# Three moves in SP's order: the store, the loads and the products of the blocked logits transposes

## The chip, the cores and the metric

One core of a Trainium2 chip runs the whole kernel. The metric is device time in microseconds, the median of three runs; smaller is better.

## The reference

Three stages follow one another on 4608 tokens of 512 features.

```
attn:  block-causal softmax(q k^T / 8) v,     8 batches, 8 heads, 576 positions, head size 64
moe:   x = relu(x @ w_in)**2 @ w_out          w_in 512 x 2048, w_out 2048 x 512
moe2:  logits = x @ phi                       phi 512 x 32
       d = softmax of logits over the tokens;  slot_input = d.T @ x
       slot_out[e] = relu(slot_input[e] @ w1[e]) @ w2[e]     8 experts, 4 slots each
       out = softmax of logits over the slots @ slot_out
```

The change touches only the path from x to logits: phi must be multiplied with x turned so that features lie on partitions, and x comes out of the second stage with tokens on partitions.

## The kernel before, in words

The program is written by hand, and a planner in `Program.order` (lines 98 to 226) sets the order of all instructions of the five engines from costs, due times and dependences. The semaphores that make an engine wait come from the data alone. An entry in `after=` binds the planner's order and adds no wait on the chip. SP issues every DMA, in one queue and in order: an instruction of SP that waits for a semaphore holds all DMAs behind it.

The second stage works on 12 chunks of 384 tokens (`CH`), and on each chunk in 16 slots, one for each 128 columns of w_in. The slots are counted through, and from chunk 2 on chunk c has slots 16c to 16c+15. A slot has two halves on TensorE. In H (line 821, `slot_h`) 12 products of 384 columns go to the bank `HB`: eight with the high part of the weight, `W`, and four with the low part, `WL`. ScalarE and VectorE then make relu, square and a split into `MG`. In O (line 846, `slot_o`) nine products of 512 columns add to three banks. TensorE does H of slot s and then O of slot s-1. The high parts stay in memory. The low parts are loaded anew for each slot from `wlo_d` (line 813, 512 KB) into one of three buffers, slot s into buffer s mod 3. Such a load waits until O of slot s-3 has used the buffer.

Attention for the batches to come runs between these slots: its loads are lines 438 (`aR<-in_kq`) and 439 (`aR<-in_v`), its products lines 452 and 506.

When a chunk is complete, `moe2` (line 872) works out its logits and softmax. For chunks 2 to 9 (`blocks`, line 885), eight chunks that are called blocks here, the turn is made so: VectorE turns 32 x 32 pieces of `X2` into `XB` (line 891), SP stores `XB`, 768 KB, to `xt_d` in HBM (line 894), and four loads of 192 KB bring it back into `YA` (line 897), which puts the pieces in place. Then come the product with phi (line 923), two small transposes of its result (line 953) and a product with x (line 976). The end of a chunk's slots is followed by slot 16(c+1), called s here. Before, the product stands behind the first H product of slot s+4, held there by the generator's one `yield` (line 915), to which the driver sends the slot's number (lines 1054 to 1065).

From the last block on (s = 160), SP's order also has loads of the weights of the third stage, 512 KB each (line 1173): first into free parts of `aR` and `aF`, where attention is finished. `XB` lies in `aF` too.

```
XB = L0.F[:, 2 * PH_:2 * PH_ + NTT * DM].rearrange("p (t n) -> p t n", t=NTT)
```

Of the kernel before, what the change touches and what calls it, by code (L numbers as in the profile page):

```python
# [21 lines left out]
NTT = CH // 128  # L22
# [236 lines left out]
def c_tr(n):  # L259
    return 100 + 1.08 * n  # L260
# [6 lines left out]
def emit(tc, qk, v, vd, kq2, v2, w, phi, w1, w2, jsel, gsel, out):  # L267
# [35 lines left out]
    YA = cp.tile([128, NTT * DM], F32, name="YA")  # L303
# [80 lines left out]
    def idle(keys):  # L384


        return [x for k in keys for x in list(pr.readers.get(k, ())) + ([pr.last_w[k]] if k in pr.last_w else [])]
# [391 lines left out]
    def x_split(c):  # L779
        r0 = CH * (c % 3)  # L780
        for k in range(KT):
            src = xv[:, k, r0:r0 + CH]
            evs = [("x", k, t) for t in range(c * CH // 64, (c + 1) * CH // 64)]
            pr.add([("dve", c_cp(CH), lambda k=k, src=src: dve.tensor_copy(xh[k], src)),
                    ("act", c_act(CH, True), lambda k=k, src=src: act.copy(xh[k], src))],
                   w=[("xh", k)], due=-1, waits=evs, sets=("xs", c, k), cls="xh")
            pr.add(("dve", c_tt(CH), lambda k=k, src=src: dve.tensor_sub(xl[k], src, f(xh[k]))),
                   r=[("xh", k)], w=[("xl", k)], due=-1, waits=evs, sets=("xs", c, k))
# [5 lines left out]
    h_at = {}  # L794
# [13 lines left out]
    def slot_h(s, due, after=()):  # L808
        c, ft = slots[s]
        i = s % 3  # L810
        wl, lk = lo(s)
        if lk[0] == "WL" and (ft not in DIRECT or s != first_use[ft]):
            pr.add(("sp", 50, lambda: sp.dma_start(f(WL[i]), wlo_d[ft])), r=[("wd", ft)],
                   w=[("WL", i, 0), ("WL", i, 1)], due=due - 9.0, nbytes=1 << 19)
        n = 0
        h_at[s] = len(pr.ops)
        for k in range(KT):
            sl = slice(k * 128, (k + 1) * 128)
            for a, b_, rk in (("h", xh[k], ("xh", k)), ("l", xh[k], ("xh", k)), ("h", xl[k], ("xl", k))):
                wk = lk + (0,) if a == "l" else ("W", ft, 0)  # L820
                pr.add(("pe", c_mm(CH), lambda a=a, b_=b_, sl=sl, n=n: pe.matmul(  # L821
                    HB[:, 0:CH], (wl() if a == "l" else W[ft])[:, sl], b_, start=(n == 0), stop=(n == 3 * KT - 1))),
                    r=[wk, rk], w=["HB"], due=due, after=after if n == 0 else ())
                n += 1
        j = s % 2
        r_, gh, gl = R2[j], GHs[j], GLs[j]
        pr.add(("act", c_act(CH), lambda: act.activation(r_, HB[:, 0:CH], AF.Relu)), w=["HB", ("r", j)], due=-1)  # L827
        pr.add([("act", c_act(CH, True), lambda: act.activation(r_, r_, AF.Square)),  # L828
                ("dve", c_tt(CH), lambda: dve.tensor_mul(r_, r_, r_))], w=[("r", j)], due=-1, cls="sq")
        pr.add([("dve", c_cp(CH), lambda: dve.tensor_copy(gh, r_)), ("act", c_act(CH, True), lambda: act.copy(gh, r_))],  # L830
               r=[("r", j)], w=[("gh", j)], due=-1, cls="gh")
        pr.add(("dve", c_tt(CH), lambda: dve.tensor_sub(gl, r_, f(gh))), r=[("r", j), ("gh", j)], w=[("gl", j)], due=-1)  # L832
# [39 lines left out]
    def moe2(c, m, due):  # L872

        z = m % 2
# [4 lines left out]
        def k2(nm, o=0):  # L879
            return (nm, (z + o) % 2)  # L880
# [4 lines left out]
        blocks = 2 <= m < NCH - 2  # L885
        if blocks:
            XB = L0.F[:, 2 * PH_:2 * PH_ + NTT * DM].rearrange("p (t n) -> p t n", t=NTT)
            oldF = idle([("a", "PT", x) for x in range(NPT // 64)] + [("a", "V"), ("a", "VD")])

            for t in range(NTT):  # L890
                pr.add(("dve", c_tr(512), lambda t=t: dve.transpose(
                    XB[:, t].rearrange("p (j k n) -> p j k n", j=4, k=KT), X2[t].rearrange("p (k j n) -> p j k n", k=KT, j=4))),
                    r=[("X2", t)], w=[("a", "XB", t)], due=due, after=oldF)
            pr.add(("sp", 50, lambda: sp.dma_start(xt_d[z].rearrange("t p n -> p t n"), XB)), r=[("a", "XB", t) for t in range(NTT)],
                   w=[("xd", z)], due=due, nbytes=3 << 18)
            for j in range(4):
                pr.add(("sp", 50, lambda j=j: sp.dma_start(
                    YA[32 * j:32 * j + 32].rearrange("p (g x) -> p g x", g=4 * NTT),
                    xt_d[z].rearrange("t (g p) (j x) -> j p (t g) x", g=4, j=4)[j])), r=[("xd", z)],
                    w=[("YA", t) for t in range(NTT)] if j == 0 else [("YAj", j)], due=due, nbytes=3 << 16)  # L900
        for t in range(0 if blocks else NTT):
            g = Group("w")
            for k in range(KT):
# [5 lines left out]
            def tb(g):  # L909
# [2 lines left out]
            pr.add([("act", c_act(512), lambda g=g, d_=d_: act.copy(d_, tb(g))),  # L912
                    ("dve", c_tt(512), lambda g=g, d_=d_: dve.tensor_copy(d_, tb(g)))],
                   w=[("YA", t)], grp=g, give=True, due=due)
        slot = (yield) if blocks else None
        g = Group("w")
        for k in range(KT):
            def mm(k=k, g=g):
                for t in range(NTT):
# [6 lines left out]
                   after=(h_at[slot],) if blocks and k == 0 else ())  # L926
        M, nM, sE = T("M"), T("nM"), T("sE")
        lg = g
        if m == 0:
            pr.add(("dve", c_tt(128), lambda: dve.reduce_max(M, bank(lg)[0:96, 0:128], axis=AX.X)),  # L930
                   w=[k2("M")], grp=g, due=due)
        else:
            mc = T("mc")
            pr.add(("dve", c_tt(128), lambda: dve.reduce_max(mc, bank(lg)[0:96, 0:128], axis=AX.X)),
                   w=[k2("mc")], grp=g, due=due)
# [8 lines left out]
        else:  # L944
            al = T("al")
            pr.add(("act", 188, lambda: act.activation(al, T("M", 1), AF.Exp, bias=nM)), r=[k2("M", 1), k2("nM")],
                   w=[k2("al")], due=due)
# [42 lines left out]
    def t_at(s):  # L990
        return T0 + TS * s
# [40 lines left out]
    def dec(ft, due, after=()):  # L1032
        w_load(ft, due - 6)
        if ft in DIRECT:
            i = first_use[ft] % 3
            w_decode(ft, due, (lambda: WL[i], ("WL", i)), after)
        else:
            i = NEAR.get(ft, FT - 2 + ft % 2)
            w_decode(ft, due, (lambda: W[i], ("W", i)), after)
# [3 lines left out]
    nxt, m, part = 3, 0, None  # L1043
# [6 lines left out]
    for s, (c, ft) in enumerate(slots):  # L1050
        if s == 0 or slots[s - 1][0] != c:
            x_split(c)
        slot_h(s, t_at(s), () if s else swapped)
        if s and slot_o(s - 1, t_at(s) + 2):
            g_ = moe2(slots[s - 1][0], m, t_at(s) - 20)
            next(g_, None)
            part = (s + 4, g_)
            m += 1

        if part and s == part[0]:  # L1060
            try:
                part[1].send(s)
            except StopIteration:
                pass
            part = None
        while nxt < FT and s >= max([dec_at[nxt]] + [FT // 2 + x + 1 for x in NEAR if NEAR[x] == nxt]):
            if nxt == FT - 4:
                swapped = (pr.add(("sp", 0, swap2), after=swapped + tuple(x for j in range(2) for x in pr.readers[("XR", j)]),
                                  due=-1),)
            dec(nxt, t_at(dec_at[nxt]) - 5, swapped)  # L1070
            nxt += 1
    slot_o(NS - 1, t_at(NS))
    list(moe2(NCH - 1, NCH - 1, 0))


# [68 lines left out]
    def rk(i):  # L1144
        return ("room", i)
# [50 lines left out]
    due = TE + 100  # L1196
# [6 lines left out]
    z = (NCH - 1) % 2  # L1203
# [18 lines left out]
    for j in range(2):  # L1222
        g2 = Group("w")
        for k in (2 * j, 2 * j + 1):
# [7 lines left out]
               w=[("sin", j)], r=YAK, grp=g2, give=True, due=due)  # L1232
# [17 lines left out]
    for g in range(2):  # L1250
        for k in range(KT):
            for n in range(2):
                def mm(g=g, k=k, n=n):
                    for j in range(4):
# [3 lines left out]
                       w=[E1k[g][n]], due=due)  # L1258
# [10 lines left out]
        for n in range(2):  # L1269
            gr = Group("w")  # L1270
            for j in range(4):
# [6 lines left out]
                   w=[hTk[g], ("hT", g, n)], grp=gr, give=True, due=due)  # L1278
# [23 lines left out]
    for h, cl in enumerate(HALF):  # L1302
        gr = Group("w")
        for k in range(4):
            for n in range(2):
# [10 lines left out]
               w=[("sob", 1, h), rk(rX2)], grp=gr, give=True, due=due + h)  # L1316
# [14 lines left out]
    for q in range(NQ):  # L1331
# [11 lines left out]
        for t in range(4):  # L1343
# [5 lines left out]
               w=[("cT", q)], grp=gr, give=True, due=due_c, after=idle([rk(CR + q // 2)]))  # L1349

    s3 = [None]
    for h, cl in enumerate(HALF):
# [6 lines left out]
        def s_hi(gc=gc, cl=cl):  # L1359
            if s3[0] is None:  # L1360
# [5 lines left out]
               w=[("s3", h)], grp=gc, give=True, due=due + h)  # L1366
# [65 lines left out]
def build(tc, **aps):  # L1432
    with tc.manual_schedule():
        emit(tc, **aps)
# [54 lines left out]
```

## Time and profile before

| what | value |
|---|---|
| median of 3 runs | 1209.64 us (1207.76 to 1210.83) |
| the profiled execution's own time | 1212.57 us |
| its span in the trace | 1210.8 us |
| TensorE's granted clock, mean | 0.986 |
| TensorE (PE) busy | 1155.0 us (95%) |
| VectorE (DVE), ScalarE (ACT) busy | 735.0 us, 658.2 us |
| DMA | 222.99 MB, mean 184 GB/s |

All durations come from the profiled execution, whose own time is 2.93 us over the median of the runs. The time outside the span is 1212.57 - 1210.8 = 1.8 us. Times in the rows count from the start of the span. A line of the timeline gives start and duration of a run of equal instructions and, in brackets, how long the engine was idle before it and who ended that.

### The profile page before, as it was taken

The numbers are of one execution on the slowest core, as the hardware profiler recorded it, in microseconds if no ns is written. First come the engines' busy times: TensorE is split into PE (matmuls) and PEld (weight loads), VectorE is DVE, ScalarE is ACT, GpSimd is POOL, SyncE is SP. The second block draws the span as 40 slices with busy tenths as digits, with TensorE's granted clock in tenths as the row PEclk, the third lists the DMA queues.
The fourth block names the chain that finished last, engine by engine and source line by source line (L and its number), as shares of the span: only waits on it lengthen the run. The fifth ranks groups of instructions, "written<-read, shape, count | busy, mean of one in ns | idle before, by whom it ended". The sixth has DMA issues, their size and how long they took to land.

```text
span 1210.8 us, 27916 instructions
## 1 busy us (share of the span) xinstructions
PE 1155.0 (95%) x10967; PEld 963.6 (80%) x10967; DVE 735.0 (61%) x2273; ACT 658.2 (54%) x2087; POOL 3.0 (0%) x16
## 2 busy tenths in 40 slices
PE   5897999999999999999999999999999999999994
PEld 4675778888888788888888888888888887988843
DVE  7999899867556656556657556566566552232213
ACT  7787687766545455455546555455555452232234
POOL 0000000000000000000000000000000000000000
PEclk9999899999999999999999999999999999999998
DMA  6597457543344545446446345446345348367898
GB/s 202 170 315 237 150 176 258 185 158 130 127 145 158 153 140 161 143 144 192 131 133 190 127 145 180 144 137 188 130 142 164 121 167 303 122 223 247 316 388 325
DMA packets 93315, 222.99 MB, mean 184 GB/s; under 512 B 14720, under 2 KB 39040, under 8 KB 93184
## 3 DMA queue, kind: packets, MB, share of 16 engines
q1 hardware_dynamic: 93184, 221.21, 54.5%
q8 instruction: 86, 1.41, 0.5%
q14 instruction: 45, 0.37, 0.1%
HBM read 196.27 MB, written 24.90 MB: 183 GB/s over the span
## 4 chain that ended last, share of the span: by engine, by line
PE 83%; DMA 6%; DVE 6%; ACT 2%; issue 1%; SPq 0%; ACTq 0%; DVEq 0%
PE HB L821 31%; PE O L846 31%; PE B L452 6%; PE B L506 5%; DMA WL<-wlo_d 3%; PE B L603 1%; PE B L923 1%; PE B L678 1%; PE O L1256 1%; PE B L705 1%; DVE anm L626 1%; PE B L976 1%; DMA aF<-in_qk 1%; DMA part_d<-X 1%; DVE aR L569 1%
## 5 line engine op out<-in xcount | busy, mean ns | idle before, releaser
L821 PE MATMUL HB<-MX,W 128*128 128x384 f32 x1568 | 439.9, 344 | 4.5 <-ACT R L827 2.6
L846 PE MATMUL O<-W,MG 128*128 128x512 f32 x1176 | 343.5, 399 | 2.0 <-DVE MG L830 1.9
L821 PEld LDWEIGHTS HB<-MX,W 128*128 128x128 f32 x1568 | 286.5, 189 | 22.6 <-issue 6.8
L821 PE MATMUL HB<-MX,WL 128*128 128x384 f32 x736 | 251.2, 341 | 4.9 <-DMA WL<-wlo_d 4.8
L846 PEld LDWEIGHTS O<-W,MG 128*128 128x128 f32 x1176 | 216.2, 188 | 41.5 <-issue 4.0
L468 ACT ACTIVATE aF<-B,aF 128x192 f32<-128x192 f32 (+8 forms) x432 | 166.4, 417 | 79.5 <-DVE aF L463 70.5
L827 ACT ACTIVATE R<-HB 128x384 f32<-128x384 f32 x192 | 94.6, 493 | 185.4 <-PE HB L821 185.3
L461 DVE TENSOR_REDUCE aF<-B 128x1 f32<-128x192 f32 (+8 forms) x432 | 110.6, 316 | 130.6 <-PE B L452 130.3
L846 PE MATMUL O<-WL,MG 128*128 128x512 f32 x552 | 160.2, 396 | 0.0
L830 DVE CAST MG<-R 128x384 fp32r<-128x384 f32 x144 | 51.4, 357 | 166.0 <-ACT R L828 164.2
L821 PEld LDWEIGHTS HB<-MX,WL 128*128 128x128 f32 x736 | 138.9, 189 | 15.5 <-DMA WL<-wlo_d 7.0
L846 PEld LDWEIGHTS O<-WL,MG 128*128 128x128 f32 x552 | 104.1, 189 | 25.3 <-issue 1.1
L832 DVE TENSOR_TENSOR MG<-R,MG 128x384 fp32r<-128x384 f32 x192 | 105.8, 551 | 10.5 <-ACT MG L830 2.6
L468 ACT ACTIVATION_READ_ACCUMULATOR aF<-B,aF 128x1 f32 x432 | 98.5, 229 | 0.0
L498 DVE STREAM_TRANSPOSE aF<-aF 128x256 f32<-128x256 f32 (+8 forms) x216 | 96.5, 486 | 0.8 <-ACT aF L494 0.5
L828 ACT ACTIVATE R<-R 128x384 f32<-128x384 f32 x165 | 87.0, 527 | 3.5
L452 PE MATMUL B<-aR 64*32 64x192 f32 (+8 forms) x3456 | 74.7, 301 | 0.0
L452 PEld LDWEIGHTS B<-aR 64*32 64x32 f32 x3456 | 54.8, 105 | 17.3 <-issue 7.3
L506 PEld LDWEIGHTS B<-aF,aR 64*64 64x64 f32 x1728 | 52.1, 133 | 19.0 <-issue 9.4
L494 ACT ACTIVATE aF<-aF 128x256 f32<-128x256 f32 (+3 forms) x144 | 55.5, 436 | 21.2 <-DVE aF L488 21.2
L506 PE MATMUL B<-aF,aR 64*64 64x192 f32 (+8 forms) x1728 | 66.9, 302 | 0.0
L519 ACT COPY xr<-B 128x288 f32<-128x288 f32 x48 | 16.8, 404 | 91.9 <-PE B L506 91.9
(258 smaller groups left out, 1166.3 us busy)
## 6 DMA issues: line engine op xcount, KB each, us to landing
WL<-wlo_d SPq DMA_DIRECT2D x179, 512.0 KB, 3.3
aR<-in_kq SPq DMA_DIRECT2D x24, 576.0 KB, 3.9
aR<-in_v SPq DMA_DIRECT2D x24, 576.0 KB, 3.8
Wr<-in_w SPq DMA_DIRECT2D x16, 512.0 KB, 4.5
aF<-in_w SPq DMA_DIRECT2D x13, 512.0 KB, 7.5
xt_d<-aF SPq DMA_DIRECT2D x8, 768.0 KB, 3.7
YA<-xt_d SPq DMA_DIRECT2D x32, 192.0 KB, 4.5
YA<-in_w SPq DMA_DIRECT2D x11, 512.0 KB, 4.4
```

The costliest lines, as they stand in the source:

```text
L452: pe.matmul(bank(gs[h])[32 * g:32 * g + 32, c:c + 32 * i + 32].rearrange("p (b n) -> p b n", n=32), x[:, S + 64 * i + 32 * q_:S + 64 * i + ...
L461: pr.add(("dve", c_tt(n), lambda g=gs[h], n=n, c=c, x=x: dve.reduce_max(St[:, 0, x:x + 1], bank(g)[:, c:c + n], axis=AX.X, negate=True)), ...
L468: pr.add(("act", c_act(n, ext=2), lambda g=gs[h], n=n, c=c, x=x, i=i, h=h: act.activation(P_(i)[:, h], bank(g)[:, c:c + n], AF.Exp, bias=S ...
L494: act.activation(P_(i)[:, h], P_(i)[:, h], AF.Copy, scale=fct[:, x + h:x + h + 1])
L498: pr.add(("dve", c_tr(2 * n), lambda i=i: dve.transpose(P_(i), P_(i))), w=[K("P2", i, h) for h in range(2)])
L506: pe.matmul(bank(gs[q_])[64 * h:64 * h + 64, 32 * k:288].rearrange("p (i n) -> p i n", n=32), v_2()[sl, h, 64 * k:64 * k + 64], L0.F[sl, o ...
L821: pr.add(("pe", c_mm(CH), lambda a=a, b_=b_, sl=sl, n=n: pe.matmul(HB[:, 0:CH], (wl() if a == "l" else W[ft])[:, sl], b_, start=(n == 0), ...
L827: pr.add(("act", c_act(CH), lambda: act.activation(r_, HB[:, 0:CH], AF.Relu)), w=["HB", ("r", j)], due=-1)
L828: pr.add([("act", c_act(CH, True), lambda: act.activation(r_, r_, AF.Square)), ("dve", c_tt(CH), lambda: dve.tensor_mul(r_, r_, r_))], w=[ ...
L830: pr.add([("dve", c_cp(CH), lambda: dve.tensor_copy(gh, r_)), ("act", c_act(CH, True), lambda: act.copy(gh, r_))], r=[("r", j)], w=[("gh", ...
L832: pr.add(("dve", c_tt(CH), lambda: dve.tensor_sub(gl, r_, f(gh))), r=[("r", j), ("gh", j)], w=[("gl", j)], due=-1)
L846: pr.add(("pe", c_mm(512), lambda a=a, b_=b_, sl=sl, t=t, p_=p_: pe.matmul(OB[t], a[:, sl], (wl() if b_ == "l" else W[ft])[:, 512:1024], s ...
```

## The change

The generator `moe2` yields three times: the store is bound behind the first H product of slot s+2, the four loads behind that of slot s+4, the product behind that of slot s+6. `yield n` tells the driver how many slots after s it wants to be called again. No operation is added or removed.

```diff
+            slot = yield 2
             pr.add(("sp", 50, lambda: sp.dma_start(xt_d[z].rearrange("t p n -> p t n"), XB)), r=[("a", "XB", t) for t in range(NTT)],
-                   w=[("xd", z)], due=due, nbytes=3 << 18)
+                   w=[("xd", z)], due=due, nbytes=3 << 18, after=(h_at[slot],))
+            slot = yield 4
             for j in range(4):
                 pr.add(("sp", 50, lambda j=j: sp.dma_start(
...
-                    w=[("YA", t) for t in range(NTT)] if j == 0 else [("YAj", j)], due=due, nbytes=3 << 16)
+                    w=[("YA", t) for t in range(NTT)] if j == 0 else [("YAj", j)], due=due, nbytes=3 << 16,
+                    after=(h_at[slot],))
...
-        slot = (yield) if blocks else None
+        slot = (yield 6) if blocks else None
...
             g_ = moe2(slots[s - 1][0], m, t_at(s) - 20)
-            next(g_, None)
-            part = (s + 4, g_)
+            part = [s, g_, next(g_, None)]
             m += 1
-        if part and s == part[0]:
+        if part and part[2] and s == part[0] + part[2]:
             try:
-                part[1].send(s)
+                part[2] = part[1].send(s)
             except StopIteration:
-                pass
-            part = None
+                part = None
```

SP in the first block, before (WL_85, WL_86 and WL_87 are the three buffers of the low parts; YA is written by four loads):

```order
L813 DMA WL_86<-wlo_d 128x1024
L813 DMA WL_87<-wlo_d 128x1024
L894 DMA xt_d<-aF 128x3x512
L813 DMA WL_85<-wlo_d 128x1024
L897 DMA YA<-xt_d 32x12x128 x4
L813 DMA WL_86<-wlo_d 128x1024
L813 DMA WL_87<-wlo_d 128x1024
L439 DMA aR_2082<-in_v 128x1152
```

The same place, changed:

```order
L813 DMA WL_86<-wlo_d 128x1024
L813 DMA WL_87<-wlo_d 128x1024
L813 DMA WL_85<-wlo_d 128x1024
L895 DMA xt_d<-aF 128x3x512
L813 DMA WL_86<-wlo_d 128x1024
L813 DMA WL_87<-wlo_d 128x1024
L899 DMA YA<-xt_d 32x12x128 x4
L439 DMA aR_2082<-in_v 128x1152
```

The store has moved behind one low-part load and the four loads behind two more. The other six blocks before the last are moved alike, with an attention load in between in some.

SP in the last block, before (aF and aR written from in_w are the weights of the third stage):

```order
L813 DMA WL_85<-wlo_d 128x1024
L1173 DMA aR_2082<-in_w 128x1024 x2
L894 DMA xt_d<-aF 128x3x512
L813 DMA WL_86<-wlo_d 128x1024
L897 DMA YA<-xt_d 32x12x128 x4
L813 DMA WL_87<-wlo_d 128x1024
L1173 DMA aF<-in_w 128x1024 x7
L813 DMA WL_85<-wlo_d 128x1024
L1173 DMA aF<-in_w 128x1024
L813 DMA WL_86<-wlo_d 128x1024
L1173 DMA aF<-in_w 128x1024
L813 DMA WL_87<-wlo_d 128x1024
```

The same place, changed:

```order
L813 DMA WL_86<-wlo_d 128x1024
L895 DMA xt_d<-aF 128x3x512
L813 DMA WL_87<-wlo_d 128x1024
L1174 DMA aF<-in_w 128x1024 x6
L813 DMA WL_85<-wlo_d 128x1024
L1174 DMA aF<-in_w 128x1024
L899 DMA YA<-xt_d 32x12x128 x4
L1174 DMA aF<-in_w 128x1024
L813 DMA WL_86<-wlo_d 128x1024
L1174 DMA aF<-in_w 128x1024
L813 DMA WL_87<-wlo_d 128x1024
```

Here the loads of YA have moved behind seven weight loads, six of which stand ahead of WL_85 where seven stood; ahead of the last WL_86 the set of transfers is the same as before.

PE in the last block, changed (W_627 is the weight of slot 165, W_628 that of slot 166; before, the product L923 stood behind the first H product of slot 164, with W_626):

```order
L821 MATMUL HB<-MX,WL_85 128x384
L821 MATMUL HB<-MX,W_627 128x384
L821 MATMUL HB<-MX,W_628 128x384
L926 MATMUL B_72<-YA,ph 32x128 x12
L846 MATMUL O_65<-W_627,MG 128x512
L846 MATMUL O_66<-W_627,MG 128x512
L846 MATMUL O_67<-W_627,MG 128x512
L846 MATMUL O_65<-WL_85,MG 128x512
L956 MATMUL B_71<-ident,LE 128x96
L821 MATMUL HB<-MX,WL_86 128x384
L821 MATMUL HB<-MX,W_628 128x384
L956 MATMUL B_71<-ident,LE 128x96
```

The product with phi now stands behind the first H product of slot 166, two slots later, and four products of O of slot 165 follow it before the first use of WL_86.

## Rows read from the trace of the kernel before

**Rows 1.** The page's part 1: busy time, share of the span, instructions.
```profile
PE 1155.0 (95%) x10967; PEld 963.6 (80%) x10967; DVE 735.0 (61%) x2273; ACT 658.2 (54%) x2087; POOL 3.0 (0%) x16
```

**Rows 2.** Windows: busy us of PE, PEld, DVE, ACT, POOL; PEclk, DMA share, GB/s.
```profile
1010.00:1020.00 10.00, 7.61 (x38) 5.29 (x37) 2.91 (x11) 2.61 (x9) 0.00 (x0) 1.00 1.03 417
```

**Rows 3.** Waits: engine line waited for, us in total, times, longest.
```profile
PEld HB L821 <- DMA WL<-wlo_d: 7.0, 7, 2.8
...
PE HB L821 <- DMA WL<-wlo_d: 4.8, 3, 2.4
```

**Rows 4.** Waits of SP's queue, same columns.
```profile
SPq L894 <- DVE aF L891: 20.9, 7, 3.4
SPq L897 <- DMA xt_d<-aF: 14.6, 7, 2.9
```

**Rows 5.** Timeline of SP in the first block: the store and the four loads.
```profile
389.90 0.37 SPq L894 DMA_DIRECT2D xt_d<-aF  x1
...
393.52 2.53 SPq L897 DMA_DIRECT2D YA<-xt_d  x4
```

**Rows 6.** Timeline of PE in the first block, at the product with phi.
```profile
400.78 1.07 PE L923 MATMUL B<-YA,ph 128*32 128x128 f32 x24 [0.30 <-DMA YA<-xt_d]
401.79 0.45 PE L821 MATMUL HB<-MX,WL 128*128 128x384 f32 x1
```

**Rows 7.** Timeline of PE, the one stall on WL between the blocks.
```profile
687.69 0.45 PE L821 MATMUL HB<-MX,WL 128*128 128x384 f32 x1 [0.44 <-DMA WL<-wlo_d]
```

**Rows 8.** Timeline of SP in the last block.
```profile
996.27 0.38 SPq L894 DMA_DIRECT2D xt_d<-aF  x1
999.29 0.33 SPq L813 DMA_DIRECT2D WL<-wlo_d  x1
1001.30 1.86 SPq L897 DMA_DIRECT2D YA<-xt_d  x4
1003.48 0.34 SPq L813 DMA_DIRECT2D WL<-wlo_d  x1
1003.91 4.31 SPq L1173 DMA_DIRECT2D aF<-in_w  x7
1008.98 0.33 SPq L813 DMA_DIRECT2D WL<-wlo_d  x1
1010.15 0.33 SPq L1173 DMA_DIRECT2D aF<-in_w  x1
1014.48 0.33 SPq L813 DMA_DIRECT2D WL<-wlo_d  x1
```

**Rows 9.** DMA issues: us to landing; WL at 999.29, 1003.48, 1008.98, 1014.48.
```profile
WL<-wlo_d SPq DMA_DIRECT2D x1, 512.0 KB, 3.5
...
WL<-wlo_d SPq DMA_DIRECT2D x1, 512.0 KB, 5.4
...
WL<-wlo_d SPq DMA_DIRECT2D x1, 512.0 KB, 10.8
...
WL<-wlo_d SPq DMA_DIRECT2D x1, 512.0 KB, 7.7
```

**Rows 10.** Timeline of PE in the last block: first H products, O, and the stalls.
```profile
1003.98 0.33 PE L821 MATMUL HB<-MX,W 128*128 128x384 f32 x1
...
1008.17 0.34 PE L821 MATMUL HB<-MX,W 128*128 128x384 f32 x1
...
1012.02 1.06 PE L976 MATMUL B<-X,ET 128*32 128x512 f32 x6
...
1016.54 0.86 PE L846 MATMUL O<-W,MG 128*128 128x512 f32 x3
1019.79 0.44 PE L821 MATMUL HB<-MX,WL 128*128 128x384 f32 x1 [2.39 <-DMA WL<-wlo_d]
...
1022.57 0.44 PE L821 MATMUL HB<-MX,W 128*128 128x384 f32 x1 [0.58 <-ACT R L827]
...
1026.86 0.34 PE L821 MATMUL HB<-MX,W 128*128 128x384 f32 x1
```

## The prediction, made before the changed kernel ran

> **What bounds the kernel now.** I read the page first: TensorE is busy for 95% of the span [rows 1]. Then the waits. All the idle time of the H products behind a low-part load is 4.8 us in three waits, and 7.0 us on the weight-load side, which largely lies beside running products [rows 3]. So what SP delivers late costs TensorE little. Then I asked where these waits stand. In the seven blocks before the last, the timeline of TensorE shows one wait that belongs to the blocked transposes, 0.30 us for YA in the first block [rows 6], and between the blocks one stall on a low part, 0.44 us [rows 7]. The largest, 2.39 us, is in the last block [rows 10]. The third wait of rows 3 is the remainder, 4.8 - 0.44 - 2.39 = 1.97 us, before the blocks begin, where nothing changes. So on these rows the place that can move the time is the last block; the rest can give back 0.74 us at most.
>
> SP itself waits much more: 20.9 us for the turned pieces before the store, and 14.6 us for the store's landing before the loads, each in seven of eight blocks, so 3.0 and 2.1 us a time [rows 4]. In the first block, 3.25 us lie between the end of the store's issue and the loads [rows 5]. Behind these waits stand low-part loads. But each of those is issued as soon as its buffer is free and is needed two slots later, which is 2 x 4.19 us (a slot is 1008.17 - 1003.98 [rows 10]), and an undisturbed one lands in 3.5 us [rows 9]. The slack of nearly 5 us covers either wait. That is why so much waiting on SP shows as so little on TensorE.
>
> **The change part by part.**
>
> *The store, one low-part load later, seven blocks.* The waits of about 3 us for VectorE go: the load now ahead of the store waits for TensorE longer than VectorE takes. All of that lay beside TensorE's work: 0 us. If that cover were gone (a low part needed sooner than 3.5 us after issue), up to 3 us a block would have been visible before, and the rows show none.
>
> *The four loads, two low-part loads later, seven blocks.* The waits of 2.1 us for the store go as well, again 0 us. The loads take 1.86 to 2.53 us of SP [rows 5, 8], as before, and now delay a later low part. The slack of 5 us covers it: 0 us.
>
> *The product, two slots later, seven blocks.* By the order the loads are issued at least 2 slots, 8.4 us, before the product. In the last block of before they are issued within 1.86 us and the next transfer had landed 7.6 us after the first issue (1003.48 + 5.4 - 1001.30 [rows 8, 9]). So YA is there. The 0.30 us of the first block goes: **-0.3 us**. The product itself takes 1.0 us of TensorE wherever it stands (400.78 to 401.79 [rows 6]), so moving it costs 0 us. Its neighbours change kind (attention products, H, O), and the order has 77 changes into another tile shape where it had 79; I price that at 0 and bound it by 0.5 us either way, half of one product.
>
> *The attention loads* stand one low-part load earlier or later in four blocks. The stall at 687.69 is behind such a load. I leave it at 0 and bound it by its own 0.44 us either way.
>
> *The last block.* Before: the low part of slot 165 (WL_85) was issued at 1008.98 behind seven weight loads, landed at 1019.78, and stalled TensorE for 2.39 us [rows 8 to 10]. The transfers are in step: from the landing of WL_87 at 1008.88 to that of WL_85 at 1019.78 eight transfers of 512 KB passed, 1.36 us each, and the DMA share is 1.03, so there is no room [rows 2, 9]. From 999.29 on, the changed order gives, with H and O half a slot each, 2.1 us (12 x 384 and 9 x 512 columns are alike):
>
> - Slots 162 and 163 are untouched, and slot 164 starts at 1008.17. Without the product, H ends at 1010.3, O of 163 at 1012.4. One H product of 165, then O of 164, end at 1014.7.
> - WL_85 lands when. At most one weight load sooner than before, 1019.78 - 1.36 = 1018.4. At best WL_87, no longer behind YA, lands 3.5 us after issue as the load at 999.29 did [rows 9], at 1007.0, and seven transfers follow: 1016.5. I take **1016.5**, as the store ahead of it is issued by 1000.0.
> - So TensorE still stalls, 1.8 us. The rest of H of 165 ends at 1018.4. With the 0.58 us for ScalarE that the row at 1022.57 shows [rows 10], the first H product of 166 is done at 1019.2.
> - Now the product waits for YA, which stands behind WL_85 and one weight load. Four loads of YA and one of 512 KB took from 1002.8 (999.29 + 3.5) to 1008.9, 6.1 us, so YA takes at most 4.7 us of the DMA engines, and no less than the 1.86 us of its issue; I take the middle, 3.3. YA lands at 1016.5 + 1.4 + 3.3 = **1021.2**. A new wait of 2.0 us takes the old one's place.
> - Product to 1022.2, four of the nine O products to 1023.1. WL_86 comes two transfers behind YA, at 1021.2 + 2 x 1.36 = 1023.9, where it came at 1022.2 before (1014.48 + 7.7 [rows 8, 9]): a wait of 0.8 us. Then 1.9 us for the eleven H products, 1.06 for the product with x [rows 10], 0.2 for the small transposes, 1.2 for the last five O products, 4.4 in all: slot 167 starts at 1028.3.
>
> Before, it started at 1026.86 [rows 10]. The term is **+1.4 us**. Its ends: with WL_85 at 1018.4 and YA at 4.7 us, YA lands at 1024.5 and WL_86 at 1027.2; slot 167 then starts at 1031.5, **+4.6 us**. With nothing left to wait for, the 2.39 and 0.58 us go: **-3.0 us**.
>
> The page "DMA: Bandwidth & Descriptors" of the Trainium skill (section "Anatomy of one DMA") fits a DMA as a fixed 2.0 us plus its bytes at 436 GB/s. By that the 786 KB of YA would take an estimated 1.8 us of transfer, near the lower end of my bounds; YA would land at 1019.7, WL_86 at 1022.4, slot 167 would start at 1026.8, and the last term would be -0.1 us. The 6.1 us measured for YA with one low part speak for the longer time.
>
> **Sum.** -0.3 + 1.4 = +1.1 us on the profiled execution's 1212.57 us, 1213.7. That execution is 2.9 us over the median of the runs shown, so for the median 1209.64 + 1.1 = **1210.7 us**.
>
> **The rivals.**
>
> *Faster, the last block runs clear.* WL_85 comes early, YA before it is missed, and both stalls go, with the 0.30 and the 0.44: 3.0 + 0.74 = 3.7 us, **1205.9 us**. For it: one weight load fewer stands ahead of WL_85, and the SP waits are gone. Against it: the engines are full in this stretch [rows 2], so an order can only exchange who is late, and TensorE arrives 2.6 us earlier than before at the place where it needs WL_85, since the product, the transposes and the product with x are no longer ahead of it.
>
> *Slower, YA is stuck behind the weights.* The YA loads of the last block now stand behind seven weight loads in a full queue, and the product holds TensorE, which takes instructions in order, with WL_86 behind YA. Each us by which YA lands later than 1021.2 is a us of stall. At its upper end the term is +4.6, with the -0.3 **1213.9 us**. It counts as slower, by over 3.6 us in all, from YA landing at about 1023.7 on. For it: the landing time grew to 10.8 us here [rows 9]. Against it: it wants both upper bounds at once.
>
> *The change does not do what it says.* The planner could have put the waits elsewhere: the loads of YA might still wait on SP for the store. By the order, two low-part loads stand between them, each waiting for a slot of TensorE, over 4 us; the first block's loads went out 3.6 us after the store [rows 5]. The time would then be as before, **1209.6 us**. It falls within no change.
>
> **How the numbers follow.** A measurement of this kernel can tell about 0.3% from no change, 3.6 us. My forecast, the last block's term between -2.5 and +3.9 us with nothing else, has 0.74; the change without effect 0.05; the slower rival 0.14; the faster 0.07. So no change has 0.79. The range for 8 in 10 takes the forecast's case whole, and on the upper side half of the slower rival: from 1209.64 - 0.3 - 2.5 = 1206.8, with the 0.5 us for the changed neighbours left out, to 1209.64 - 0.3 + 4.2 = 1213.5.
>
> **What would show it right or wrong.** Right: SP's waits at the store and at the loads (20.9 and 14.6 us) nearly gone, with TensorE's idle time in the seven blocks still under 1 us; no wait before the product in the first block; in the last block a wait for WL_85 shorter than 2.39 us and a new one of 1 to 3 us before the product, for YA, and slot 167 starting 1 to 2 us later, against slot 164, than the 18.7 us of before. Wrong: stalls on WL in the seven blocks, which would mean that the slack is thinner than two slots; a product that finds YA there in the last block; or a change of over 1 us before 990 us of the span, where I have -0.3.

## The result: slower by 0.6%, most of it in the last block

The changed kernel takes 1216.55 us in the median of 16 runs (1212.63 to 1223.44), the kernel before 1209.63 in 16 runs (1205.63 to 1216.03). The ratio is 1.0061, with a 95% interval of 1.0046 to 1.0076, some 5.6 to 9.2 us. Forecast were 1210.7 us and a range up to 1213.5.

The two profiled executions hide this: their spans are equal, 1210.8 us. That is the luck of the draw: the changed kernel's, 1212.63 us, is the fastest of its 16 runs, and that of before, 1212.57 us, lies 2.9 us over its median. The page's first lines of the changed kernel answer to [rows 1]:

```profile
PE 1153.1 (95%) x10967; PEld 961.7 (79%) x10967; DVE 734.3 (61%) x2274; ACT 657.4 (54%) x2086; POOL 3.0 (0%) x16
```

One relu (line 827) belongs to each of the 192 slots, so the starts of these instructions on ScalarE give a clock of the program that both kernels share. Here is its timeline at slots 48 (ahead of the first block), 160 (start of the last block) and 168 (behind it), first before, then changed.

```profile
385.71 0.51 ACT L827 ACTIVATE R<-HB 128x384 f32<-128x384 f32 x1
...
994.97 0.49 ACT L827 ACTIVATE R<-HB 128x384 f32<-128x384 f32 x1 [0.94 <-PE HB L821]
...
1033.35 0.49 ACT L827 ACTIVATE R<-HB 128x384 f32<-128x384 f32 x1 [3.14 <-PE HB L821]
```

```profile
379.64 0.52 ACT L827 ACTIVATE R<-HB 128x384 f32<-128x384 f32 x1
...
990.67 0.49 ACT L827 ACTIVATE R<-HB 128x384 f32<-128x384 f32 x1 [0.94 <-PE HB L821]
...
1033.38 0.49 ACT L827 ACTIVATE R<-HB 128x384 f32<-128x384 f32 x1 [3.14 <-PE HB L821]
```

The changed execution was 6.07 us ahead at slot 48, where nothing has been changed yet; at slot 160 it was 4.30 us ahead, at slot 168 0.03 us behind. So the change cost 6.1 us in this pair, and the start of the program happened to give back the same. The stretches of all profiled executions of this study, in us, from differences of such starts:

```
execution                 slots 8-24   24-48   48-160   160-168   168-191
before                       109.59   139.90   609.26     38.38    101.28
changed                      105.48   139.84   611.03     42.71    101.26
e1 last block as before      105.83   139.94   609.81     38.70    101.34
e2 last block alone          105.83   139.92   609.30     42.45    100.95
e3 loads free                105.13   139.92   615.76     39.24    102.28
e4 product alone             105.00   139.90   612.46     44.00    102.15
e5 changed, weights later    107.36   139.90   610.61     34.90    102.20
e6 before, weights later     105.57   139.84   608.87     34.90    102.69
e7 changed, busy ahead       107.17   139.84   609.43     41.73    100.96
e8 changed again             109.47   139.85   609.55     43.58    101.80
```

Slots 8 to 24, which no change touches, differ by 4.6 us, and most of that is one late low part near 229 us. Before and e8 stall there for 1.97 and 2.00 us and then have a granted clock of 0.50 for some 3 us (109.6 and 109.5 us in these slots); e7 and e5 stall for 2.13 and 1.31 us at the full clock (107.2 and 107.4); the others have no such stall over 0.3 us (105.0 to 105.8).

In slots 48 to 160, the seven blocks before the last, the five executions with the change's order have 609.43 to 611.03, mean 610.1; the three with the order of before 608.87 to 609.30, mean 609.1: +0.9 us, where executions of one order differ by up to 1.6 us. In slots 160 to 168 the three with the change in the last block (changed, e2, e8) have a mean of 42.9, the two without it 38.5: +4.4 us. Together 5.3 us, a little under the interval, which begins at 5.6.

**The last block after the change.** SP's queue, to be held against [rows 8]:

```profile
999.55 3.21 SPq L1174 DMA_DIRECT2D aF<-in_w  x6
...
1003.38 0.33 SPq L813 DMA_DIRECT2D WL<-wlo_d  x1
...
1004.77 5.80 SPq L899 DMA_DIRECT2D YA<-xt_d  x4
...
1011.18 0.38 SPq L813 DMA_DIRECT2D WL<-wlo_d  x1
...
1014.87 0.32 SPq L813 DMA_DIRECT2D WL<-wlo_d  x1
```

SP no longer waits for the turned pieces or for the store's landing, but the loads now sit in a full queue: their issue alone takes 5.80 us, where it took 1.86. The last of the four started at 1008.5, and its row among the DMA issues gives 10.2 us to landing, so YA was there at 1018.7:

```profile
YA<-xt_d SPq DMA_DIRECT2D x1, 192.0 KB, 10.2
```

TensorE, to be held against [rows 10]; the first line is the start of slot 164, the last that of slot 167:

```profile
1003.88 0.34 PE L821 MATMUL HB<-MX,W 128*128 128x384 f32 x1
...
1012.37 0.44 PE L821 MATMUL HB<-MX,WL 128*128 128x384 f32 x1 [1.87 <-DMA WL<-wlo_d]
...
1015.14 0.44 PE L821 MATMUL HB<-MX,W 128*128 128x384 f32 x1 [0.58 <-ACT R L827]
...
1018.77 1.91 PE L926 MATMUL B<-YA,ph 128*32 128x128 f32 x24 [3.18 <-DMA YA<-xt_d]
...
1020.60 1.65 PE L846 MATMUL O<-W,MG 128*128 128x512 f32 x3
...
1026.88 0.34 PE L821 MATMUL HB<-MX,W 128*128 128x384 f32 x1
```

The stall on WL_85 is 1.87 us where it was 2.39; a new one of 3.18 us for YA stands before the product; and the product takes 1.91 us where it took 1.07, the three O products behind it 1.65 where such three take 0.86. Slot 164 to slot 167 is 23.0 us where it was 18.7. The windows show the reason for the long products (columns as in [rows 2]):

```profile
1014.00:1016.00 2.00, 1.01 (x5) 0.43 (x3) 0.32 (x1) 1.01 (x2) 0.00 (x0) 1.00 1.23 206
1016.00:1018.00 2.00, 0.00 (x0) 0.00 (x0) 0.60 (x2) 0.00 (x0) 0.00 (x0) 1.00 1.16 214
1018.00:1020.00 2.00, 1.23 (x18) 1.17 (x21) 0.00 (x0) 0.00 (x0) 0.00 (x0) 0.71 0.99 377
1020.00:1022.00 2.00, 2.00 (x15) 1.36 (x7) 0.59 (x3) 0.85 (x4) 0.00 (x0) 0.50 1.05 424
1022.00:1024.00 2.00, 2.00 (x13) 1.46 (x14) 0.73 (x3) 0.31 (x3) 0.00 (x0) 0.94 0.24 92
```

Behind the wait of 3.18 us the granted clock fell to the lower of its two levels (1.2 instead of 2.4 GHz, shown as 0.50) and stayed there for about 3 us. The missing clock of the last three rows is 2 x (0.29 + 0.50 + 0.06) = 1.7 us of work at the full clock.

**SP's waits and the seven blocks.** The waits of SP for the store's source and for the store's landing, 20.9 and 14.6 us in [rows 4], are gone; what is left at the two lines is small:

```profile
SPq L899 <- DMA aF<-in_w: 3.1, 4, 0.9
SPq L895 <- DVE MG L832: 1.4, 3, 0.5
SPq L895 <- DVE aF L463: 0.5, 1, 0.5
```

TensorE gained nothing from it. It has new stalls on a low part in the third and sixth block; here is the third, on SP and on PE, with the landing time of the low part issued at 571.72:

```profile
570.19 0.33 SPq L438 DMA_DIRECT2D aR<-in_kq  x1
...
571.72 0.39 SPq L813 DMA_DIRECT2D WL<-wlo_d  x1
...
572.16 1.97 SPq L899 DMA_DIRECT2D YA<-xt_d  x4
```

```profile
576.41 0.34 PE L821 MATMUL HB<-MX,W 128*128 128x384 f32 x1
...
577.52 0.45 PE L821 MATMUL HB<-MX,WL 128*128 128x384 f32 x1 [0.77 <-DMA WL<-wlo_d]
```

```profile
WL<-wlo_d SPq DMA_DIRECT2D x1, 512.0 KB, 5.8
```

The low part stands behind an attention load and is followed at once by the loads of YA. It takes 5.8 us, and TensorE wanted it 5.0 us after its issue.

### The profile page after: what moved, and what is told of

Its sections match the earlier page's. It is cut to its first block, busy times and chain, and to the rows that moved or that the text cites. A ratio compares the mean times of both kernels' runs of the same rounds, so it can differ in the third digit from the quotient of the medians.

```text
span 1210.8 us, 27909 instructions
## 1 busy us (share of the span) xinstructions
PE 1153.1 (95%) x10967; PEld 961.7 (79%) x10967; DVE 734.3 (61%) x2274; ACT 657.4 (54%) x2086; POOL 3.0 (0%) x16
## 4 chain that ended last, share of the span: by engine, by line
PE 84%; DVE 7%; DMA 5%; ACT 2%; issue 1%; SPq 0%; ACTq 0%; DVEq 0%
PE HB L821 31%; PE O L846 31%; PE B L452 6%; PE B L506 5%; DMA WL<-wlo_d 1%; PE B L926 1%; DVE anm L626 1%; PE B L678 1%; PE B L603 1%; PE B L979 1%; PE B L705 1%; PE O L1257 1%; DMA YA<-xt_d 1%; DVE aR L569 1%; DMA aF<-in_qk 1%
```

## Experiments

Two theories at first. **A**: the loads of YA come late in the last block, behind the weights of the third stage, and two of the seven blocks lose a little to a late low part. **B**: the product itself costs more at its new place on TensorE, in each block. Each run is compared with the kernel before on the same chip.

### e1: the seven blocks alone

The generator goes the new way unless the block is the last (`m == NCH - 3`), which keeps store, loads and product as before.

```diff
+            new = m != NCH - 3
-            slot = yield 2
+            slot = (yield 2) if new else None
-                   w=[("xd", z)], due=due, nbytes=3 << 18, after=(h_at[slot],))
-            slot = yield 4
+                   w=[("xd", z)], due=due, nbytes=3 << 18, after=(h_at[slot],) if new else ())
+            slot = (yield 4) if new else None
-                    after=(h_at[slot],))
+                    after=(h_at[slot],) if new else ())
-        slot = (yield 6) if blocks else None
+        slot = (yield 6 if new else 4) if blocks else None
```

> The change in the seven blocks before the last, the last block as before. Theory A (the loads of YA, bound to slot s+4, come behind the weights of the third stage in the last block, where two thirds of the loss lie; the seven other blocks lose about 1.8 us, in two of them, where an attention load and YA surround a low-part load that has under 2 us to spare): 1.8 us over before, ratio 1.0015, with stalls on WL of 0.8 and 1.4 us in the third and sixth block and the last block's stall on WL at 2.4 us as before. Theory B (the product with phi, two slots later on TensorE, costs about 0.9 us in each block): 6 us over before, ratio 1.005, with no single stall that explains it.

Measured: 1210.63 us against 1211.28, ratio 0.9998 (0.9979 to 1.0017). Slots 48 to 160 took 609.81 us, 160 to 168 38.70. The stall of the last block is as before, by the row of PE:

```profile
1015.27 0.44 PE L821 MATMUL HB<-MX,WL 128*128 128x384 f32 x1 [2.70 <-DMA WL<-wlo_d]
```

Theory B falls: seven moved products cost nothing that can be measured. The stalls on WL in the third and sixth block are there (0.76 and 0.64 us), but worth less in sum than the 1.8 us expected.

### e2: the last block alone

As e1 with `new = m == NCH - 3`.

> The change in the last block alone. Theory A: 4.3 to 5 us over before, ratio 1.004, with a wait for YA of about 3 us before the product in the last block and a granted clock of half for some 3 us behind it. Theory B: 0.9 us over before, ratio 1.0007.

Measured: 1215.99 us, ratio 1.0033 (1.0015 to 1.0051). Slots 48 to 160 are as before to 0.04 us (609.30), slots 160 to 168 took 42.45 us. The wait for YA on PE, and the granted clock behind it:

```profile
1020.99 1.93 PE L927 MATMUL B<-YA,ph 128*32 128x128 f32 x24 [3.00 <-DMA YA<-xt_d]
```

```profile
1022.00:1024.00 2.00, 2.00 (x18) 1.38 (x13) 0.59 (x3) 0.59 (x3) 0.00 (x0) 0.50 1.04 420
```

So the last block alone makes the loss, with the wait and the low clock that theory A wanted.

### e3: loads right behind the store

Store at s+2 and product at s+6, no bound on the four loads.

```diff
-            slot = yield 4
...
-                    after=(h_at[slot],))
+                    after=())
```

> The store bound to s+2 and the product to s+6 in all eight blocks; the four loads follow the store as the planner puts them, in the last block ahead of the weights of the third stage. Theory A: no wait for YA in the last block, no stalls over 0.5 us in the seven blocks, time within 2 us of before, ratio 0.9985 to 1.0015. Theory B: the product stands where the change put it, so the whole loss stays, 6.9 us, ratio 1.006.

Measured: 1215.53 us, ratio 1.0052 (1.0029 to 1.0075). This meets the number of B and the place of neither. In the last block YA is there and the stretch is 39.24 us, 0.7 over before, as A had it. The loss lies in slots 48 to 160: 615.76 us, 6.6 over the mean of before's order, with six stalls on low parts that add up to 5.2 us. Four of them stand at the first low-part product of slot s+4, which the product stood directly ahead of before the change [rows 6]. The largest, and the granted clock behind it:

```profile
748.66 0.44 PE L821 MATMUL HB<-MX,WL 128*128 128x384 f32 x1 [1.66 <-DMA WL<-wlo_d]
```

```profile
750.00:752.00 2.00, 2.00 (x8) 1.91 (x7) 1.77 (x3) 0.17 (x1) 0.00 (x0) 0.50 0.93 154
```

The low level lasted some 3 us, 1.7 us of work at the full clock. With the stalls that makes 6.9 us, about the loss.

Here SP waits for the store's landing again, with low parts behind it, as in [rows 4]:

```profile
SPq L898 <- DMA xt_d<-aF: 19.2, 8, 5.3
```

Before, such waits of SP cost TensorE next to nothing. What differs on TensorE is the product, which no longer stands in slot s+4. SP's waits stand one low part later too, so this run alone does not separate the two.

### e4: the product alone

Store and loads unbound, as before; product at s+6. In the last block SP's order is that of before. In four of the other blocks the planner now puts one attention load one place earlier or later, 15 to 23 us behind where the product stood, and on TensorE attention products move by up to a slot along with the product.

> The product alone bound to s+6; store and loads where they stood before the change. Theory A: nothing in the seven blocks; in the last block WL of slot 165 lands as before and the 2.6 us of product, small transposes and product with x that stood ahead of that stall now stand behind it: 2.3 us over before, ratio 1.002. Theory B: 6.9 us over before, ratio 1.006.

Measured: 1218.50 us, ratio 1.0061 (1.0041 to 1.0080), as slow as the whole change. Five of the seven blocks have a stall of 0.6 to 0.8 us on a low part (3.6 us in all; slots 48 to 160 took 612.46, 3.3 over). All five stand at the first low-part product of slot s+4, which in [rows 6] follows the product with no wait, and each is shorter than the product's 1.07 us. The first of them, then the last block, which took 44.00 us, 5.5 over:

```profile
397.02 0.44 PE L821 MATMUL HB<-MX,WL 128*128 128x384 f32 x1 [0.79 <-DMA WL<-wlo_d]
...
1009.00 0.45 PE L821 MATMUL HB<-MX,WL 128*128 128x384 f32 x1 [1.55 <-DMA WL<-wlo_d]
...
1019.00 0.44 PE L821 MATMUL HB<-MX,WL 128*128 128x384 f32 x1 [3.47 <-DMA WL<-wlo_d]
...
1023.04 1.93 PE L924 MATMUL B<-YA,ph 128*32 128x128 f32 x24
```

```profile
1022.00:1024.00 2.00, 1.57 (x16) 1.15 (x19) 0.92 (x2) 0.90 (x2) 0.00 (x0) 0.50 0.20 74
```

In the last block YA is in time, and WL_85 lands when it did. But TensorE now comes to it without having done the product, the small transposes and the product with x. It stalls for 1.55 and 3.47 us instead of 2.39, then still has that work to do, and does it at half the clock: the four windows of 2 us from 1020 on have 0.57, 0.50, 0.50 and 0.73, at most 3.4 us of work lost. A had 2.3 us for this; the rest is the low clock and the seven blocks.

So a **theory C**: the product and the work behind it were filling for low parts that came late. In the seven blocks that is the product's own 1.07 us in slot s+4, and the low parts came late by SP's waits; in the last block it is 2.6 us in slot 164, with the small transposes and the product with x, and the low part of slot 165 came late by the weights ahead of it. Moving the work away uncovers them. The change's later loads then take the SP waits away in the seven blocks (which wins back 2.4 of e4's 3.3 us there), but in the last block they put YA itself behind the weights. If C holds, the place of the product is worth nothing once the last block's queue is free.

### e5: the change, with the weights out of the way

The nine weight loads into `aF` are bound eleven slots later, one to a slot from slot 168 on.

```diff
-            aft = {h_at[min(NS - NFR + n, NS - 1)]}
+            aft = {h_at[min(NS - NFR + n + (11 if 3 <= n < 12 else 0), NS - 1)]}
```

> The changed kernel with the nine weight loads of the third stage into aF bound eleven slots later, one to a slot behind the last block's product, so that the DMA queue is free in the last block. Theory C (the product and what follows it, 2.6 us of TensorE, were work to do while the low part of slot 165 was late; two slots later they are not, YA comes late behind the weights, and TensorE then runs at half clock for a while; all of it hangs on the nine weight loads): no stall over 0.6 us between slots 160 and 168 and no clock below full there; that stretch is 3.0 us shorter than before's and 7 us shorter than the changed kernel's, the time 1 to 2.5 us under before, ratio 0.998 to 0.9995. Theory B (the product's place costs by itself): the loss of the last block stays, ratio 1.004 or more.

Measured: 1208.16 us against 1210.16, ratio 0.9986 (0.9972 to 1.0001). The last block took 34.90 us. The product meets YA, at full clock:

```profile
1016.09 1.07 PE L926 MATMUL B<-YA,ph 128*32 128x128 f32 x24
```

Theory C had 1 to 2.5 us less than before, and this is 2.0, though the interval just reaches no change. B's 1.004 lies outside it.

### e6: before, with the weights out of the way

The same edit in the kernel before.

> The kernel before with the same nine weight loads eleven slots later. Theory C: the last block's stall of 2.39 us and the wait of 0.58 us go, 3.0 us under before, ratio 0.9975. If the stall has another cause than the weights in the queue, it stays and the ratio is 1.000.

Measured: 1206.71 us, ratio 0.9965 (0.9954 to 0.9977), faster than both kernels. The last block again took 34.90 us, 3.5 less than before's 38.4: with the product at s+4 or at s+6, the stretch is the same to 0.01 us as soon as the weights are out of the way, so there the product's place costs nothing. Later the nine loads cost little: slots 168 to 191 took 102.69 us, 1.4 more than before and with a stall of 0.51 us on a low part, where the executions with these loads in their old place have 100.95 to 102.28; the whole is still 0.35% less. The change itself remains no gain: e5 is 1.45 us over e6 in the medians and 1.7 us in slots 48 to 160, which is not clear of the spread.

### e7: TensorE kept busy ahead of the product

```diff
             def mm(k=k, g=g):
+                if m == NCH - 3 and k == 0:
+                    for _ in range(28):
+                        pe.transpose(bank(g)[:, 256:384], ident, ident)
                 for t in range(NTT):
```

> The changed kernel with 28 transposes of the identity, some 3 us of work for nothing, ahead of the last block's product, where TensorE waits 3.2 us for YA. Theory C: the wait lasts as long, but TensorE's granted clock stays full behind it, the product takes 1.07 us instead of 1.91, and the stretch from slot 160 to 168 is about 1.6 us shorter than in the changed kernel. If the low clock has another cause, the stretch is as long or longer.

Measured: 1213.60 us, ratio 1.0029 (1.0014 to 1.0044), where the changed kernel beside it (e8) had 1.0049. The timeline of PE, then the windows:

```profile
1017.76 3.22 PE L924 MATMUL B<-ident 128*128 128x128 f32 x28
...
1020.91 1.07 PE L929 MATMUL B<-YA,ph 128*32 128x128 f32 x24
...
1023.71 0.44 PE L821 MATMUL HB<-MX,WL 128*128 128x384 f32 x1 [0.52 <-DMA WL<-wlo_d]
```

```profile
1018.00:1020.00 2.00, 2.00 (x21) 2.00 (x20) 0.92 (x2) 0.00 (x0) 0.00 (x0) 1.00 1.19 211
1020.00:1022.00 2.00, 2.00 (x34) 1.63 (x32) 0.00 (x0) 0.00 (x0) 0.00 (x0) 1.00 0.98 373
```

The clock stays full and the product takes 1.07 us, as expected. The stretch is 41.73 us, 1.0 under the first execution of the changed kernel and 1.2 under the mean of the three without this work; 1.6 were expected. The next transfer, WL_86, has become the limit: a stall of 0.52 us stands where the slow products had hidden it.

### e8: the changed kernel again

> The changed kernel once more, beside the others on their chip. The stretch from slot 160 to 168 is again 4.3 us longer than before's, within 0.3 us; the start of the span, up to slot 48, where nothing is changed, differs by some us from run to run.

Measured: 1216.94 us, ratio 1.0049 (1.0035 to 1.0062). The last block took 43.58 us, 5.2 over before, so the 0.3 us allowed were too few: the clock fell earlier, behind the stall on WL_85, and stayed low up to about 1029.

```profile
1024.61 1.93 PE L926 MATMUL B<-YA,ph 128*32 128x128 f32 x24 [2.51 <-DMA YA<-xt_d]
```

```profile
1020.00:1022.00 2.00, 1.42 (x4) 0.61 (x3) 0.05 (x1) 1.01 (x2) 0.00 (x0) 0.50 1.27 222
1026.00:1028.00 2.00, 2.00 (x13) 1.34 (x8) 0.62 (x4) 0.90 (x4) 0.00 (x0) 0.50 0.88 352
```

Slots 8 to 24 took 109.47 us here and 105.48 in the first execution of the same kernel.

## Why the prediction was wrong, point by point

- **Where it would be decided**: right. The last block makes 4.4 of the 5.3 us that the stretches show, and the mechanism is the rival "YA is stuck behind the weights", which had 0.14. Its price, 1213.9 us, was short as well. The sum had +1.4 us for this block; from slot 164 to slot 167 the changed execution takes 4.3 us more than before. Two steps failed there: YA's time in the queue and the clock.
- **The stall on WL_85** in the last block: 1.8 us forecast, 1.87 measured.
- **YA's time in the queue** was mis-sized. From the landing of WL_85 to that of YA the sum has 4.7 us: 1.4 for a weight load and 3.3, the middle of 1.9 and 4.7, for YA. WL_85 landed at 1012.4 and YA at 1018.7, 6.4 us later. With the weight load at its 1.36 that leaves 5.0 us for YA, above my upper end; the two overlapped in the queue (the weight load itself landed at 1014.8), so only their sum is measured. Counted from slot 164, YA landed 1.8 us later than forecast, and the wait for it was 3.18 us, not 2.0. The windows show why: in the stretch of YA the DMA engines are full at 206 to 214 GB/s, where the weights run at 418 to 424. The estimate by the Trainium skill's page "DMA: Bandwidth & Descriptors" (section "Anatomy of one DMA"), 1.8 us, was further off than the row that I had beside it: the measurement decides, and these loads run at half the rate of that fit, which the page gives for DMAs issued on the GpSimd path, while these go out on SP.
- **The clock** was missing from the sum, which takes every duration at the full clock and gives no reason for it. In the last block of before, a stall of 2.39 us had left the granted clock at 1.00. In the changed kernel's last block the low clock cost 1.7 us of work at the full clock, and e7 gets 1.0 to 1.2 us of it back. The trace of before has that price too: the third wait of [rows 3], 1.97 us, was followed by the lower level for some 3 us.

```profile
229.47 0.44 PE L821 MATMUL HB<-MX,WL 128*128 128x384 f32 x1 [1.97 <-DMA WL<-wlo_d]
```

```profile
230.00:232.00 2.00, 2.00 (x10) 2.00 (x9) 1.55 (x6) 1.26 (x2) 0.00 (x0) 0.62 0.16 53
232.00:234.00 2.00, 2.00 (x7) 1.77 (x7) 1.46 (x5) 1.00 (x4) 0.00 (x0) 0.53 0.00 0
```

- **"The product itself takes 1.0 us of TensorE wherever it stands, so moving it costs 0 us"** failed too. At the full clock its length did not change with its place; what it covered did. e4 moves it with SP's order all but kept, and loses 3.3 us in the seven blocks and 5.5 in the last. In the changed kernel this step matters less: in the seven blocks the SP waits that the product covered are gone as well, and for the last block the forecast's own timeline already lets TensorE come to WL_85 without this work and does it behind YA.
- **The slack of "nearly 5 us"** of the low parts was mis-sized, and with it the zero for the seven blocks. I let a low part be needed two slots after its issue. Its buffer is freed in the O half of slot s-3, which TensorE does at the end of slot s-2, so little more than one slot is left: 5.0 us from issue to need in the third block, and 1.5 us to spare over the undisturbed 3.5. Forecast were -0.3 us, measured +0.9, with stalls on low parts, above all in the third and sixth block: the first of the prediction's own signs of being wrong. With SP's waits left in place and the product gone (e3, e4) it was +6.6 and +3.3.
- **SP's waits**: right that they would go and that TensorE would not gain by it.
- Of the difference of the medians, 6.9 us, the stretches explain 5.3. The interval of the result begins at 5.6 us, that of e8, the same kernel, at 4.2. What the remainder is stays open.

## What to carry to other kernels

When an instruction moves on the engine that sets the time, ask what it was filling: work that stands just ahead of a late transfer costs nothing there, and elsewhere can cost up to its length (0.6 to 0.8 of 1.07 us in five blocks of e4). Count a prefetch's slack from the instruction that frees its buffer to the one that needs it, in the order in which the engine does them. And where a burst of early loads fills the queue, moving the burst may be worth more than any reordering around it: here one line (e6) made the kernel before 0.35% faster, since its nine loads were issued from 1003.9 on and the first product that reads from them starts at 1148.0.

## What the runs showed of the hardware

- Loads with pieces of 128 numbers (YA, 512 bytes each, four loads to 32 partitions each) kept the DMA engines full at 206 to 214 GB/s, half of what the 4 KB rows of the weights reach (418 to 424 GB/s). Whether the short pieces or the few partitions make the difference, no run separates.
- The length of a stall alone did not tell whether TensorE's clock fell. Single stalls of 2.39 and 2.70 us in the last block (before, e1) and of 2.13 us near 229 us (e7) left it at 1.00. Single stalls of 1.97 us near 229 us (before), 1.66 us (e3), 1.88 us (e8) and 3.47 us (e4, 6.5 us behind one of 1.55) were followed by the lower level, about 1 us after work had begun again. In the changed kernel it fell at the end of the wait of 3.18 us, which came 3 us behind the stall of 1.87. The lower level then lasted some 3 us (before, the changed kernel, e3), 7 us (e4) and 10 us (e8).
- The start of the program, the same instructions in all kernels, varied: slots 8 to 24 took 105.0 to 109.6 us. Equal spans of two profiled executions said nothing about the change until they were compared stretch by stretch.
